# An FFT convolution on one core: the head's weight and pixel steps regrouped, and its loads reordered

## The chip, the core and the metric

The kernel runs on one core of a Trainium2 chip. The metric is the device time of one execution in microseconds; the time of the kernel before is the median of three runs. One further execution was taken with the hardware profiler, and the timelines below are from it. The engines are TensorE (PE: matrix products, with PEld for its weight loads), VectorE (DVE), ScalarE (ACT), GpSimd (POOL) and SyncE (SP), which issues the DMAs of this kernel. A "core's 16 DMA engines" move the data.

## The reference

```python
def reference(x, w):                       # x: 1 x 224 x 224 x 96, w: 7 x 7 x 96 x 96, bf16
    B, H, W, C = x.shape
    K = w.shape[0]
    wp = jnp.pad(w, ((0, H - K), (0, W - K), (0, 0), (0, 0)))
    Xf = jnp.fft.rfft2(x.astype(jnp.float32), axes=(1, 2))
    Wf = jnp.fft.rfft2(wp.astype(jnp.float32), axes=(0, 1))
    Yf = jnp.einsum('bhwi,hwio->bhwo', Xf, Wf)
    return jnp.fft.irfft2(Yf, s=(H, W), axes=(1, 2)).astype(jnp.bfloat16)
```

That is a circular convolution of a 224 x 224 picture of 96 channels with 7 x 7 weights, 96 channels in and 96 out.

## The kernel before, in words

The height is cut into NJ = 8 strips of 28 rows, which are transformed along the height only, with a short Fourier transform that gives NS = 17 frequencies (two of them, 0 and 16, are pairs of real ones: `REAL`). The strips are held in two groups (`jg`) of four, each 118 picture rows with its overlap of 6 rows. The width is cut into seven tiles of 32 pixels. Along the width the kernel convolves directly, two pixels (phases) at a time, with a scheme of ten tap planes (`NTAP`) in place of seven.

Four kinds of work follow each other:

- **Weights.** The 49 weights of every pair of channels lie in a wide SBUF tile `wq`, one weight per partition. There are two copies: rows 30 to 78 for output channels in full order, and rows 79 to 127 shifted by 48 channels, so that one matmul can serve two output channels. The matmul multiplies a strided column set of `wq` with the factor table `Em` (made at the start from a sine and masks), which gives the transformed weights in `WF`. The first group of frequencies (`wide_jobs`, L407, five frequencies in 11 slots) needs the first copy alone. The other groups (`prep_jobs`, L425, three frequencies each) need both. Each job is some matmuls into one PSUM bank and one eviction (a copy from PSUM to SBUF).
- **Pixels.** `f_jobs` (L514) transforms the pixels of the first three tiles, in three parts of the frequencies (`SH2`, 8 + 5 + 4), for each strip group; `a_bank` does the halo of three pixel pairs, and `a_jobs` the later tiles. The pixels come from DRAM by `load_rows` (L177), for each group one DMA of 112 rows (L183, `PAD` to `R`) and one of 6 rows.
- **Rounds.** `b_round` (L567) does one frequency of one tile: 33 matmuls (22 for a real frequency) on the pixel planes `xf` and the planes `J`, which DVE forms by `jit` (L536) for three frequencies at a time; then DVE and POOL combine the products into `yf`, which goes to DRAM (`scr`). The third slot of a frequency's weights is the difference of the first two (`diff`, L400, on DVE).
- **Way back.** `c_jobs` reads `scr` back into tiles `tt` (`load_t`, L673; its last group is read in parts of 64, 4 and 34 partitions), multiplies with a matrix `Gm` and stores the output.

What sets the order: each engine runs its instructions in the order in which the program writes them (`_Ordered`, L92). The head (L770 to L787) is written out by hand: 24 weight jobs of four channels, with the pixel transforms of tile 0's first part and the halo placed after the 12th, 16th and 20th, and a filler matmul (`warm`) after every fourth. The rounds follow (L828). Between the matmuls of a round other jobs are dealt out by `pace` (L795): a queue of jobs is entered with a first and a last step (`add(a, b, jobs)`), where round r of tile 0 has the steps 2r and 2r + 1. Weight group 1 is dealt from step 4 on, the second tile's first transform from step 3. `evac` (L133) gives each eviction to DVE or ACT, whichever has less by a running count.

SP issues its DMAs in order. The framework gives them eight semaphores in turn, so each DMA also waits until the eighth one before it has landed. In the head the order is (L203 to L213): the first weight copy (48 rows, then its last row in two DMAs of 16 pieces each), the first pixels of group 0, both halos, the first pixels of group 1, the second pixels of both groups, the second weight copy (48 rows in four DMAs by columns, then its last row).

Of the kernel before, what the change touches and what calls it, by code (L numbers as in the profile page):

```python
# [10 lines left out]
ALU = mybir.AluOpType  # L11
# [3 lines left out]
B = 28  # L15
L = B + KT - 1
LC = L - 2
NS = L // 2
REAL = (0, NS - 1)
JG = 4  # L20
# [8 lines left out]
NB0 = 4  # L29
# [4 lines left out]
PGRP = ((0, 5), (5, 8), (8, 11), (11, 14), (14, 17))  # L34
# [8 lines left out]
CQ = {2: (11, 0), 3: (11, 3), 4: (8, 7), 5: (4, 11), 6: (0, 11)}  # L43
SH2 = (0, 8, 13, 17)
# [3 lines left out]
FILL = 2  # L48
FEV = 4
WX0 = 12  # L50
WHALO = 16
WX1 = 20
W1 = 30
ZA = 1200
ZB = 3600
# [3 lines left out]
S5 = ((0, 1), (2, 3, 4), (5, 6, 11), (7, 8, 12), (9, 10, 13))  # L59
NW0 = 11  # L60


def slot(s, part):
    return S5[s][part] if s < len(S5) else 2 + 3 * (s - 1) + part


@with_exitstack
def kernel(
# [17 lines left out]
    assert K1 + PW == EP and len(S5) == PGRP[0][1]  # L86
# [26 lines left out]
    ps0_cm = tc.tile_pool(name="ps0", bufs=8, space=bass.MemoryType.PSUM)  # L113
    pools = {"psb": ps0_cm.__enter__()}
# [32 lines left out]
    def dma(out_ap, in_ap):  # L147
        return DE.dma_start(out=out_ap, in_=in_ap)
# [21 lines left out]
    Em = wqx[0:EP, WE:WE + 2 * NSLOT * NTAP].rearrange("p (h a t) -> p h a t", h=2, a=NSLOT)  # L170
# [6 lines left out]
    def load_rows(xb, jg, w0, npx):  # L177
        h0 = jg * HB - PAD
        n = npx * C

        def ld(p0, p1, hh):
            return dma(xb[p0:p1, 0:n], x[0, hh:hh + (p1 - p0), w0:w0 + npx, :].rearrange("h w c -> h (w c)"))
        return ld(PAD, R, h0 + PAD), ld(0, PAD, h0 % H)  # L183
# [9 lines left out]
    def load_w(p, k, n, h, m0=0, m1=C * C):  # L193
        return dma(wqx[p:p + n, m0:m1], bass.AP(wsrc.tensor, wsrc.offset + k * C * C + h * C2 + m0, [[C * C, n], [1, m1 - m0]]))

    def load_last(p, h):
        n = (C * C, WC)[h]
        m = n // 16
        for a, b in ((0, m // 2), (m // 2, m)):
            dma(wqx[p:p + 1, 0:n].rearrange("p (c m) -> p c m", c=16)[:, :, a:b],  # L200
                bass.AP(wsrc.tensor, wsrc.offset + (PW - 1) * C * C + h * C2 + a, [[C * C, 1], [m, 16], [1, b - a]]))

    load_w(W1, 0, PW - 1, 0)  # L203
    load_last(K1 - 1, 0)
# [3 lines left out]
    load_x(0, 1)  # L208
    for jg in range(2):
        load_x(1, jg)  # L210
    for i in range(4):
        load_w(K1, 0, PW - 1, 1, i * WC // 4, (i + 1) * WC // 4)
    load_last(EP - 1, 1)  # L213
# [5 lines left out]
    def warm(n):  # L219
        pwu = bank()  # L220
        for _ in range(n):
            TE.matmul(pwu[:].rearrange("p (a b) -> p a b", a=4), lhsT=wu[:, 0:128], rhs=wur, start=True, stop=True)
# [27 lines left out]
    zero_a(EP, WE // 2 + NSLOT * NTAP, 64 * C)  # L250
    zero_a(W1, 0, ZA)

# [31 lines left out]
    zero_a(W1, ZA, ZB)  # L284

    iota(twc[:], [[1, KT]])
    twp = ftile([EP, 1]); mk = ftile([EP, NTAP]); mk2 = ftile([EP, 2, NTAP])
# [7 lines left out]
    GE.memset(wz[0:W1, ZB:WE // 2], 0.0)  # L295
    GE.memset(mf[:], 1.0)
    GE.affine_select(out=mf[:], in_=mf[:], pattern=[[-B, JG], [0, NS * 2]], compare_op=ALU.is_ge, fill=0.0, base=-1, channel_multiplier=1)
    GE.affine_select(out=mf[:], in_=mf[:], pattern=[[B, JG], [0, NS * 2]], compare_op=ALU.is_ge, fill=0.0, base=LC, channel_multiplier=-1)
# [14 lines left out]
    pe3 = ftile([EP, NSLOT])  # L313
    pv = pe3[:, 2:].rearrange("p (s r) -> p s r", r=3)
    VE.tensor_copy(out=pe3[:, 0:2], in_=qe[:, 0, :])
    VE.tensor_single_scalar(out=pv[:, 0:NS - 2, 0], in_=qe[:, 1:NS - 1, 0], scalar=-2.0, op=ALU.mult)
    VE.tensor_tensor(out=pv[:, 0:NS - 2, 1], in0=qe[:, 1:NS - 1, 1], in1=qe[:, 1:NS - 1, 0], op=ALU.subtract)
    for r, k in ((0, KT - 1), (1, 0)):
        VE.tensor_single_scalar(out=pv[:, NS - 2, r:r + 1], in_=thp[:], scalar=float(k), op=ALU.is_equal)
    VE.tensor_tensor(out=pv[:, :, 2], in0=pv[:, :, 0], in1=pv[:, :, 1], op=ALU.subtract)  # L320

    def factors(h0, h1, out_ap, in_ap):
        n = list(in_ap.shape[1:])
        o, i = out_ap, in_ap.unsqueeze(len(n) + 1)
        m = mk2[:, h0:h1]
        if h1 - h0 > 1:
            i = i.unsqueeze(1)
            m = m.unsqueeze(2)
            shape = [EP, h1 - h0, *n, NTAP]
        else:  # L330
            m = m.unsqueeze(2) if len(n) > 1 else m
            shape = [EP, *n, NTAP]
        VE.tensor_tensor(out=o, in0=i.to_broadcast(shape), in1=m.to_broadcast(shape), op=ALU.mult)
    factors(0, 1, Em[:, 0, 0:5], pe3[:, 0:5])
    factors(0, 1, Em[:, 0, 5:NW0].rearrange("p (s r) t -> p s r t", r=2),
            pe3[:, 5:14].rearrange("p (s r) -> p s r", r=3)[:, :, 0:2])
    factors(0, 2, Em[:, :, NW0:], pe3[:, NW0:])
    factors(1, 2, Em[:, 1, 0:NW0], pe3[:, 0:NW0])
# [68 lines left out]
    def wide_jobs():  # L407
        ncol = NW0 * NTAP
        wcol = 512 // NB0
        assert ncol <= wcol and C % NB0 == 0  # L410

        def mk_(ob):
            def f():
                pw = bank()
                pv_ = pw[:].rearrange("p (k q) -> p k q", q=wcol)
                ev = Em[0:K1, 0].rearrange("p a t -> p (a t)")[:, 0:wcol]
                o0 = ob * NB0
                for k in range(NB0):
                    TE.matmul(pv_[:, k], lhsT=wqx[0:K1, o0 + k:o0 + k + 127 * C + 1:C], rhs=ev, start=True, stop=True)
                wv = WF[0:C, 0:NW0].rearrange("i a t o -> i (a t) o")  # L420
                apart(("W", 0), ob, evac(wv[..., o0:o0 + NB0], pv_[0:C, :, 0:ncol].rearrange("i k q -> i q k"), NB0 * ncol))
            return f
        return [mk_(ob) for ob in range(C // NB0)]

    def prep_jobs(gi):  # L425
        s0, s1 = PGRP[gi]
        ns = s1 - s0
        ncol = 2 * ns * NTAP
        nb = C // NB
        hb = NB // 2  # L430
        assert NB * ncol <= 512 and C2 % hb == 0

        def mk_(ob):
            def f():
                pw = bank()
                wv = WF[0:C, slot(s0, 0):slot(s1 - 1, 2) + 1]
                pv_ = pw[:, 0:NB * ncol].rearrange("p (k h q) -> p k h q", h=2, q=ncol)
                ev = Em[:, :, slot(s0, 0):slot(s1 - 1, 2) + 1, :]
                ev = ev.rearrange("p h (s r) t -> p h s (r t)", r=3)[:, :, :, 0:2 * NTAP]
                for k in range(hb):  # L440
                    o = ob * hb + k
                    TE.matmul(pv_[:, k], lhsT=wqx[0:EP, o:o + 127 * C + 1:C], rhs=ev, start=True, stop=True)
                pv_ = pv_[0:C]
                o0, o1 = ob * hb, (ob + 1) * hb
                wv = wv.rearrange("i (s r) t (h o) -> i s (r t) h o", r=3, h=2)
                apart(("W", gi), ob, evac(wv[:, :, 0:2 * NTAP, :, o0:o1],
                      pv_.rearrange("i k h (s q) -> i s q h k", s=ns), NB * ncol))
            return f
        return [mk_(ob) for ob in range(nb)] + [diff(s) for s in range(s0, s1) if s not in REAL]
# [64 lines left out]
    def f_jobs(t, part):  # L514
        s0, s1 = SH2[part], SH2[part + 1]
# [255 lines left out]
    fj = [f_jobs(0, p) for p in range(3)]  # L771
    warm(FILL)
    load["v"] += 900
    for i, f in enumerate(wide_jobs()):
        if i == WX0:
            for g in fj[0][0]:
                g()
        if i == WHALO:
            for jg in range(2):
                for g in a_bank(0, xf0, xh_bufs[jg], 0, 3, jg, 0):  # L780
                    g()
        if i == WX1:
            for g in fj[0][1] + jit(0, 0):
                g()
        f()
        if i % FEV == FEV - 1:
            warm(1)  # L787
# [25 lines left out]

    for gi in range(1, len(PGRP)):
        add(4 if gi == 1 else 2 * PGRP[gi - 1][0], 2 * PGRP[gi - 1][1] - 1, prep_jobs(gi))
# [12 lines left out]
    for r in range(NS + LAG):  # L828
        if r == 0:
            for i in range(2, PGRP[0][1]):  # L830
                add(2 * i - 3, 2 * i - 2, [diff(i)])
            add(1, 6, fj[1][0] + fj[1][1])
            add(6, 10, fj[2][0] + fj[2][1])
        if r == 2:
            new_xf(1, SH2[0], SH2[1])
        for p in range(3):
            if r == (1, 3, 5)[p]:
                if p:
                    new_xf(1, SH2[p], SH2[p + 1])
                else:  # L840
                    xf_tiles[1] = xf_bufs[1]
                fj = f_jobs(1, p)
                if p == 2:
                    for jg in range(2):
                        fj[jg][-1] = then_load(fj[jg][-1], 2, jg)
                add(2 * r + 1, 2 * r + (5, 5, 4)[p], fj[0] + fj[1])
# [144 lines left out]
```

## Time and profile before

| | us |
|---|---|
| median of three runs | 272.68 (270.92 to 272.82) |
| profiled execution, its time | 269.92 |
| its span | 268.2 |
| first weight matmul / first matmul of a round | 8.17 / 19.39 |
| PE's longest wait in the rounds, for the second weight copy | 2.65, up to 26.82 |
| all bytes moved by the DMA engines | 46.78 MB, 174 GB/s on average |

A line of the timeline gives the start, the duration, the engine (a "q" behind it: its instruction queue, where DMAs are issued), the line of the program, the operation, what is written and read, how many instructions were merged into the line, and in brackets the idle time before it with what ended it. All work of this kernel goes through one helper, so every line has the number L102, and groups are told apart by their tiles: `pb` is a PSUM bank, `WF` the transformed weights (the tile's end also holds the first pixels), `wq` the raw weights, `xn` the pixels, `xf` the transformed pixels, `wu` the filler. The trace also keeps, for each DMA, the times at which its semaphore was raised, and a record of every packet.

### The profile page before, as it was taken

What the parts mean: (1) busy time and instruction counts of PE and PEld (TensorE: products, weight loads), DVE (VectorE), ACT (ScalarE), POOL (GpSimd) and SP (SyncE); (2) the same over time, 40 slices, a digit from 0 to 9 for tenths busy, and PEclk for the clock granted to TensorE, in tenths of its full rate; (3) what the DMA queues carried; (4) which work ended last, traced back from release to release, by engine and by line L of the source; (5) the groups of instructions that cost most, each with busy time, mean ns of one, the idle gap of its engine ahead of it and who ended that gap; (6) DMA issues with size and microseconds to landing.
All of it is one profiled execution on the core that took longest, in us unless ns stands there. A gap on an engine that the chain in (4) does not pass through costs nothing.

```text
span 268.2 us, 12140 instructions
## 1 busy us (share of the span) xinstructions
PE 254.2 (95%) x5127; PEld 235.4 (88%) x5127; DVE 216.0 (81%) x463; ACT 198.1 (74%) x487; POOL 99.8 (37%) x153
## 2 busy tenths in 40 slices
PE   8786999999999999999999999999999999999983
PEld 2775999989998999999999998989999889879862
DVE  7896799989899788779787888787898889878614
ACT  8686897487974578988988789887987864178113
POOL 7784215363647435322322222224123332422100
PEclk9999999999999999999999999999999999999999
DMA  7995101811111598987967387979788434787866
GB/s 162 250 242 94 50 2 46 241 51 66 46 46 50 161 260 138 290 268 197 297 184 218 110 212 249 236 186 350 267 155 240 169 108 143 196 235 197 233 123 205
DMA packets 46882, 46.78 MB, mean 174 GB/s; under 512 B 35340, under 2 KB 38104, under 8 KB 46780
## 3 DMA queue, kind: packets, MB, share of 16 engines
q1 hardware_dynamic: 44540, 43.95, 59.7%
q10 hardware_dynamic: 2288, 2.06, 2.7%
q8 instruction: 40, 0.66, 1.0%
q14 instruction: 14, 0.11, 0.1%
HBM read 24.66 MB, written 21.33 MB: 171 GB/s over the span
## 4 chain that ended last, share of the span: by engine, by line
PE 66%; DMA 16%; DVE 10%; ACT 2%; issue 2%; SPq 1%; DVEq 0%; ACTq 0%
PE pb L102 66%; DVE J L102 4%; DMA scrb<-yf 4%; DMA xn<-in_x_dram 3%; DMA wq<-in_w_dram 3%; DMA WF<-in_x_dram 3%; DMA tt<-scr 2%; DVE WF L102 2%; DVE v L102 2%; DMA xf<-scrb 1%; DVE u L102 1%; ACT xf L102 1%; SPq L102 1%; DVE yf L102 0%; ACT J L102 0%
## 5 line engine op out<-in xcount | busy, mean ns | idle before, releaser
L102 PE MATMUL pb<-WF,J 96*128 96x96 bf16 x2821 | 162.7, 206 | 1.8 <-DVE J L102 1.1
L102 PEld LDWEIGHTS <-J 96*128 96x128 bf16 x2821 | 138.0, 98 | 12.1 <-issue 3.5
L102 POOL TENSOR_TENSOR yf<-v,u 128x384 bf16<-128x384 f32 x79 | 81.6, 1044 | 144.4 <-issue 84.7
L102 ACT CAST xf<-pb 96x408 bf16<-96x408 f32 (+3 forms) x146 | 67.5, 486 | 6.4 <-PE pb L102 2.7
L102 PE MATMUL pb<-WF,xf 96*128 96x96 bf16 x952 | 59.9, 206 | 1.1 <-ACT WF L102 1.1
L102 DVE TENSOR_TENSOR J<-xf 96x456 bf16<-96x456 bf16 (+3 forms) x85 | 56.8, 708 | 0.1
L102 PEld LDWEIGHTS <-xf 96*128 96x128 bf16 x952 | 47.1, 98 | 1.5 <-issue 1.4
L102 PE MATMUL pb<-Fm,xn 118*128 118x136 bf16 (+3 forms) x640 | 45.5, 199 | 0.0
L102 PE MATMUL pb<-tt,Gm 102*84 102x384 bf16 (+1 forms) x132 | 32.8, 327 | 0.2
L102 ACT CAST WF<-pb 96x480 bf16<-96x480 f32 (+1 forms) x59 | 28.7, 557 | 4.2 <-PE pb L102 4.2
L102 PEld LDWEIGHTS <-xn 118*128 118x128 bf16 x640 | 30.1, 97 | 0.0
L102 ACT CAST J<-pb 84x384 bf16<-84x384 f32 (+1 forms) x64 | 27.6, 490 | 2.6 <-PE pb L102 2.6
L102 ACT CAST yo<-pb 84x384 bf16<-84x384 f32 (+1 forms) x64 | 27.5, 487 | 2.3 <-POOL yf L102 1.3
L102 PE MATMUL pb<-wq 128*128 128x120 bf16 (+1 forms) x288 | 21.8, 226 | 4.3 <-DMA wq<-in_w_dram 2.6
L102 DVE TENSOR_TENSOR J<-J 96x912 bf16<-96x912 bf16 (+2 forms) x42 | 24.3, 579 | 0.0
L102 PEld LDWEIGHTS <-wq 128*128 128x128 bf16 (+1 forms) x288 | 19.8, 148 | 5.1 <-issue 2.8
L102 DVE TENSOR_TENSOR yf<-v,u 128x384 bf16<-128x384 f32 x26 | 14.7, 566 | 0.9
L102 PE MATMUL pb<-wu 128*112 128x384 bf16 (+1 forms) x58 | 13.8, 385 | 1.1 <-DVE J L102 1.1
L102 PEld LDWEIGHTS <-wu 128*112 128x112 bf16 (+1 forms) x58 | 7.2, 126 | 5.6 <-issue 2.8
L102 PEld LDWEIGHTS <-Gm 102*84 102x84 bf16 (+1 forms) x132 | 11.1, 117 | 0.9 <-issue 0.2
L102 ACT COPY xf<-xf 96x816 bf16<-96x816 bf16 (+3 forms) x20 | 11.1, 612 | 0.0
L102 ACT CAST tt<-pb 112x384 bf16<-112x384 f32 x8 | 3.6, 480 | 9.7 <-PE pb L102 9.5
(391 smaller groups left out, 243.4 us busy)
## 6 DMA issues: line engine op xcount, KB each, us to landing
scr<-yf SPq DMA_DIRECT2D x30, 288.0 KB
xn<-in_x_dram SPq DMA_DIRECT2D x12, 672.0 KB
tt<-scr SPq DMA_DIRECT2D x24, 336.0 KB
out_dram<-yo SPq DMA_DIRECT2D x12, 252.0 KB
out_dram<-J SPq DMA_DIRECT2D x12, 252.0 KB
tt<-scr SPq DMA_DIRECT2D x6, 288.0 KB
WF<-in_x_dram SPq DMA_DIRECT2D x2, 672.0 KB
out_dram<-tt SPq DMA_DIRECT2D x8, 168.0 KB
```

Source lines behind the costliest of these rows:

```text
L102: r = fn(*a, **k)
```

## The change

In the head, weights go in jobs of twelve channels instead of four, each into a PSUM tile of two banks with one eviction; the first weight group has four frequencies in 8 slots instead of five in 11, and the first pixel transform six frequencies instead of eight. The order of the head's steps is a list, `HEAD`, and the filler matmul goes ahead of each weight job but the first. The factor table is stored in stripes in the spare end of `wq`. The zeroing of `wq` is split by output half, all on ACT, the second half later. The second weight copy is loaded ahead of the second pixels; both copies' order changes: the last row of the first copy goes first, and the second copy is loaded in DMAs of all 49 rows. Pixel rows that do not wrap round the picture (group 1) are loaded in one DMA of 118 rows. Work that leaves the head goes into the rounds: weight groups are now 4 + 3 + 3 + 3 + 4, the last in jobs of six channels.

```diff
-NB0 = 4
+NB0 = 12
-PGRP = ((0, 5), (5, 8), (8, 11), (11, 14), (14, 17))
+PGRP = ((0, 4), (4, 7), (7, 10), (10, 13), (13, 17))
+SH0 = (0, 6, 13, 17)
+HEAD = ("w", "w", "w", "w", "x0", "w", "h0", "w", "h1", "w", "w", "x1")
...
-S5 = ((0, 1), (2, 3, 4), (5, 6, 11), (7, 8, 12), (9, 10, 13))
+S4 = ((0, 1), (2, 3, 8), (4, 5, 9), (6, 7, 10))
...
-    ps0_cm = tc.tile_pool(name="ps0", bufs=8, space=bass.MemoryType.PSUM)
+    psh_cm = tc.tile_pool(name="psh", bufs=4, space=bass.MemoryType.PSUM)
...
+        if h0 >= 0:
+            return ld(0, R, h0)
         return ld(PAD, R, h0 + PAD), ld(0, PAD, h0 % H)
...
+    load_last(K1 - 1, 0)
     load_w(W1, 0, PW - 1, 0)
-    load_last(K1 - 1, 0)
     load_x(0, 0)
     for jg in range(2):
         load_rows(xh_bufs[jg], jg, W - PAD, PAD)
     load_x(0, 1)
+    for i in range(4):
+        load_w(K1, 0, PW, 1, i * WC // 4, (i + 1) * WC // 4)
     for jg in range(2):
         load_x(1, jg)
-    for i in range(4):
-        load_w(K1, 0, PW - 1, 1, i * WC // 4, (i + 1) * WC // 4)
-    load_last(EP - 1, 1)
...
-    zero_a(EP, WE // 2 + NSLOT * NTAP, 64 * C)
-    zero_a(W1, 0, ZA)
+    zero_a(EP, WE // 2, 64 * C)
+    zero_h(0, 0, ZC)
...
+    zero_h(0, ZC, C)
+    late_zero = zero_h(1, 0, C)
...
         def mk_(ob):
             def f():
-                pw = bank()
+                pw = psum_tile()
...
+                if ob:
+                    warm(1, pw)
                 for k in range(NB0):
-                    TE.matmul(pv_[:, k], lhsT=wqx[0:K1, o0 + k:o0 + k + 127 * C + 1:C], rhs=ev, start=True, stop=True)
+                    o = ob * NB0 + k
+                    m = TE.matmul(pw[:, k // nk, k % nk * ncol:(k % nk + 1) * ncol], lhsT=wqx[0:K1, o:o + 127 * C + 1:C],
+                                  rhs=ev, start=True, stop=True)
...
+    def head_x(jg):
+        s1 = SH0[1]
+        fv = Fm[:, :, 0:s1].rearrange("p r s j -> p r (s j)")
+        n = 2 * s1 * JG
+        for ph in range(2):
+            pa = psum_tile()
+            for k in range(TW):
+                i = 2 * k + ph
+                TE.matmul(pa[:, k // 8, k % 8 * 64:k % 8 * 64 + n], lhsT=xbuf(0, jg)[:, i * C:i * C + 128], rhs=fv, start=True, stop=True)
+            xo = xf0[0:C, ph, :, 0:s1, HALO:HALO + TW, jg * JG:(jg + 1) * JG]
+            pi = pa[0:C].rearrange("c b (w q) -> c (b w) q", q=64)[:, :, 0:n].rearrange("c w (r s j) -> c r s w j", r=2, s=s1)
+            apart(("A", 0), (0, jg, ph, 0), evac(xo, pi, TW * n))
...
-        nb = C // NB
-        hb = NB // 2
+        nb = C // (NB if 2 * ncol * (NB // 2) <= 512 else 6)
+        hb = C2 // nb
...
+    wj = wide_jobs()
+    for h in HEAD:
+        if h == "w":
+            wj.pop(0)()
+        else:
+            (head_x if h[0] == "x" else head_h)(int(h[1]))
+    for g in jit(0, 0):
+        g()
...
-        add(4 if gi == 1 else 2 * PGRP[gi - 1][0], 2 * PGRP[gi - 1][1] - 1, prep_jobs(gi))
+        add(3 if gi == 1 else 2 * PGRP[gi - 1][0], 2 * PGRP[gi - 1][1] - 1, prep_jobs(gi))
...
-            add(1, 6, fj[1][0] + fj[1][1])
-            add(6, 10, fj[2][0] + fj[2][1])
+            add(0, 4, fj[1][0] + fj[1][1])
+            add(8, 12, fj[2][0] + fj[2][1])
...
-            if r == (1, 3, 5)[p]:
+            if r == (1, 3, 6)[p]:
...
-                add(2 * r + 1, 2 * r + (5, 5, 4)[p], fj[0] + fj[1])
+                add((4, 7, 12)[p], (7, 11, 15)[p], fj[0] + fj[1])
```

## The prediction, made before the changed kernel ran

> **What bounds it now.** I read the page's engine rows first, then the timeline of PE, then that of SP, then the DMA view and the trace's semaphore records.
>
> ```profile
> PE 254.2 (95%) x5127; PEld 235.4 (88%) x5127; DVE 216.0 (81%) x463; ACT 198.1 (74%) x487; POOL 99.8 (37%) x153
> q1 hardware_dynamic: 44540, 43.95, 59.7%
> 8.17 1.19 PE L102 MATMUL pb<-wq 79*128 79x128 bf16 x16 [1.62 <-POOL ct L102]
> 19.39 0.50 PE L102 MATMUL pb<-WF,xf 96*128 96x96 bf16 x8 [1.15 <-ACT WF L102]
> 26.82 0.92 PE L102 MATMUL pb<-wq 128*128 128x120 bf16 x12 [2.65 <-DMA wq<-in_w_dram]
> ```
>
> TensorE sets the time. The reader is to see in the three timeline rows when the head starts (8.17), when the rounds start (19.39), and the one long wait in the rounds: at 26.82 PE had waited 2.65 us (2.81 from the last start) for the second weight copy. After that, gaps between matmul starts, beyond the usual pitch, sum to about 5 us up to the tail. So any shift of the round start, and any new wait of PE, goes to the end in full. The DMA engines are 60% busy, with room only if the work is spread evenly. Each DMA uses the 16 engines as its shape allows, and the change alters two shapes.
>
> ```profile
> 0.80 1.70 SPq L102 DMA_DIRECT2D wq<-in_w_dram  x3
> 2.54 6.06 SPq L102 DMA_DIRECT2D WF<-in_x_dram  x8
> 10.24 1.50 SPq L102 DMA_DIRECT2D xn<-in_x_dram  x4
> 11.78 7.58 SPq L102 DMA_DIRECT2D wq<-in_w_dram  x6
> ```
>
> These are SP's issues in the head: first weights, first pixels, second pixels, second weights. The first packet leaves 1.04 us after its issue (0.80 to 1.83), and a landing is recorded about 1.1 us after its last packet (6.44 to 7.59).
>
> **The step that decides: 118 and 49 rows.** Every engine that carries a part of a DMA raises its semaphore once; where fewer than 16 do, one more rise comes at once, about 0.5 us after the issue. Counted in the trace: 112, 128 and 48 rows give 16 late rises; 84, 56 and 28 rows give 14; 18 rows 9; 12 rows 12; 6 rows 6; 4 rows 4; and the 34-row pieces of tt (L684) only 2. Each count is the largest divisor of the row number that is at most 16. The changed code loads pixel group 1 in one DMA of 118 rows (2 x 59) where L183 has 112 + 6, and the second weights in DMAs of 49 rows (7 x 7) where L212 has 48. So I take **two engines for 118 rows and seven for 49.** The two 34-row pieces, issued 0.32 us apart at 120.45, land 1.3 us apart, near the 1.4 us that 68 packets of 384 B take at 20 ns: they run one behind the other on the same two engines. The Trainium skill, "DMA: Bandwidth & Descriptors", section "Why a DMA increments its semaphore by 16 and not by 1", gives this rule (largest k up to 16 that divides the slowest dimension, on the lowest-numbered engines); the trace agrees wherever it has a row, but has none for 118 or 49.
>
> What a row costs:
>
> ```profile
> DMA packets 183, 0.99 MB, mean 283 GB/s; under 512 B 22, under 2 KB 22, under 8 KB 183
> q1 hardware_dynamic: 183, 0.99, 96.6%
> ```
>
> That is 92.5 to 96 us, mostly one pixel load: 0.99 MB in 16 x 3.5 x 0.966 engine-us is 18.3 GB/s each, 0.336 us for a row of 6144 B. From 14 to 20 us it is 1.42 MB at 99.9%, or 0.415 us a row. The packet records have 0.234 at the fast tenth. With two engines alone drawing, I take 0.25 us, near the fast end; 0.234 and 0.415 stay as bounds.
>
> **Head, on the two engines, in the new order.** The two pieces of the last weight row go first (0.64 + 0.58 us of SP), so the 48 rows are issued at about 2.1 and start at 3.1. Three packets of 1.27: 6.9. First pixels, 8 rows at 0.40: 10.1. Halos: 8 packets of 0.076, then group 1's halo, now 118 rows, 59 x 0.076 = 4.5: 15.2. First pixels of group 1: 59 x 0.25 = 14.8: 30.0, landed **31.1**. Second weights, 4 x 7 packets of 4.6 KB at 0.2 (0.184 fastest, 0.37 in the head): 35.6. Second pixels, group 0: 37.6; group 1, again 14.8: 52.4, landed **53.5**. It was 21.4 before.
>
> PE reaches the last head step (transform of group 1) about 9.2 us after its first matmul, near 18, and waits to 31.1. Then 32 matmuls at 29 ns, the last eviction of 768 elements (0.93 us by DVE's 0.64 for 512), the first J piece (0.47); the second weights are landed when the first prep job asks for them. The next stop is the fifth job of the second pixels' first transform, the first one on group 1, in step 5 of the rounds. Up to there PE has done 88 convolution matmuls x 0.043, 64 first-pixel ones x 0.028, 36 weight ones x 0.0625 and 32 second-pixel ones x 0.029: 8.8 us, and stands at about 42. It goes on at 53.5. Before, the same work (8.6 at its pitches) was done at 19.4 + 8.6 + 2.8 = 30.8. **Shift +22.7.** The bounds: 0.234 a row and every other row at its fastest end at +18.8; 0.415 and 0.37 at +47.
>
> PE after a long pause: sixteen 512-column matmuls at the start take 5.50 us, the first ten 0.427 apart, the later 0.216. A pause of 2.65 us brought no such slow run. Pauses of 9 to 13 us are not in the trace: 0 to 10 x 0.211 = 2.1 us each, so 0 to 4.2; I take **+1**, as the first pause is followed by waits on evictions anyway. The Trainium skill, "TensorE: Matmul & The Clock Gate", section "Part 1: The HAM clock gate", halves the clock after an idle window of 3.4 us, for about as long: by it, an estimate of 1.7 us each; no run here shows it yet.
>
> **Later tiles: five more 118-row loads.** The trace gives issue and first use of group 1 for the tiles after: 49.5 to 67.3, 93.1 to 109.0, 123.1 to 138.9, 157.9 to 170.8, 184.9 to 203.2: 17.9, 16.0, 15.8, 12.9, 18.3 us.
>
> ```profile
> 157.86 0.83 SPq L102 DMA_DIRECT2D xn<-in_x_dram  x2
> 170.77 0.34 PE L102 MATMUL pb<-Fm,xn 118*128 118x136 bf16 x3
> ```
>
> The new load takes 1.0 + 59 x 0.27 (a middle of the later windows) + 1.1 = 18.0. Short by 0.1, 2, 2.2, 5.1 and 0. Behind it on the same two engines stand loads of tt. For tile 2 they are issued from 96.06 and first used at 103.92; behind a load that ends at 93.1 + 17 they land at 111: 7 us instead of 2. Every DMA on SP also waits for the landing of the eighth before it, so SP stops eight issues behind a slow load; for the other three tiles I add 2 to 3 us each. Together about 0.5 + 7 + 4 + 7 + 3 = **+21.5.** Cross-check: per tile the two engines carry 59 x 0.27 in place of 8 x 0.27, 13.8 us more on some 21 now (48 store packets of 0.09, 420 gather packets of 0.022, 24 output packets of 0.12, 16 rows), 35 in periods of 28 to 33: +2 to +7 per tile. Bounds 0 (all hidden) and +40 (0.35 a row, every shortfall 5 us more).
>
> **All other edits** are covered by these waits: two-bank evictions, 12,384 elements in 14 evictions for 16,288 in 36; one weight group of four instead of three (16 evictions for 12); factors in stripes; zeroing on ACT. Their cost if the cover is gone is in rival 1. A two-bank eviction is not in the trace: a plain extrapolation gives 1.13 us (DVE) and 0.92 (ACT) for 960, a second start would add 0.13; 14 of them leave PE's wait for 31.1 as it is.
>
> **Sum.** The profiled execution took 269.92 (span 268.2). 269.9 + 22.7 + 1 + 21.5 = 315.1. It lies 2.76 below the median of the three runs, 272.68, so **318** against that median.
>
> **Rivals.** (1) The rows spread over all engines, and the change does what it says. Then the second weights land near 19 and the 2.81 wait goes. Against it: the first weights start 1.3 later with no small pieces behind them (0.45): +0.6; PE stays bound in the head, 96 weight matmuls at 0.0625 whether 120 or 128 columns, so hardly less at 80, and J now follows the last eviction: +0.8; +0.5 of PE work in the rounds, about +0.5 of new waits as 1 us per engine of evictions moves there. 272.7 - 2.8 + 2.4 = 272.3, not slower. It decides if a 118-row DMA uses eight engines or more; only the lack of such a row in the trace speaks for it. (2) Two engines, but the later loads hide: 18 us against slacks of 13 to 18 speaks for it, tt behind them against: 272.7 + 23.7 = 296. (3) Two engines at crowded pace throughout, 0.415 in the head and 0.35 later: 272.7 + 47 + 40 = 360; the busy windows speak for it, the fast tenth against.
>
> **Chances.** Forecast 0.60 (303 to 335), rival 2 0.23, rival 3 0.13, rival 1 0.04. Range: from rival 2's lower edge, 291, to 352, which leaves out most of rival 3 and all of 1. A measurement of this kernel tells about 1% from no change: slower 0.96, within 0.03, faster 0.01, the last two from rival 1.
>
> **What would show it.** Right: the 118-row loads with two late rises, group 1's first transform starting near 31 after a wait on a DMA, a second wait of about 10 us ending near 53, then waits at tt or xn once per tile; GB/s near 50 in 18 to 50 us. Wrong: sixteen rises for 118 rows, or rounds starting near 20.

## The result and the profile after

The changed kernel takes **341.0 us** (median of six runs, 339.99 to 343.31) against 272.1 (six runs, 270.92 to 273.45): a ratio of 1.254, 95% interval 1.248 to 1.260. The profiled execution took 340.27, its span is 338.5. The forecast was 318, its range 291 to 352.

The page of the changed kernel, the lines that answer to those shown of before (engine: busy time, share of the span, instructions; queue: packets, MB, share of the engines' time), and the two rows of slices (8.46 us each):

```profile
span 338.5 us, 12099 instructions
PE 272.0 (80%) x5126; PEld 250.1 (74%) x5126; DVE 215.4 (64%) x459; ACT 202.5 (60%) x474; POOL 97.3 (29%) x152
PEclk9585696999998999679999999956999699999998
GB/s 139 163 133 53 57 82 5 5 124 105 85 41 37 40 154 118 108 162 281 206 95 133 198 181 193 84 107 209 216 306 86 49 218 277 132 158 236 201 187 163
q1 hardware_dynamic: 44284, 43.95, 44.8%
```

The same two rows of the kernel before (slices of 6.71 us):

```profile
PEclk9999999999999999999999999999999999999999
GB/s 162 250 242 94 50 2 46 241 51 66 46 46 50 161 260 138 290 268 197 297 184 218 110 212 249 236 186 350 267 155 240 169 108 143 196 235 197 233 123 205
```

The same 43.95 MB go through SP's queue, but the engines are busy 44.8% of the time with it instead of 59.7%. A low rate alone says little: before, too, it is 46 to 66 GB/s where little is to be moved. New are low rates while loads are pending: 53 and 57 GB/s in the slices from 25 to 42 us. A row of 6144 B takes 0.238 us where such a load runs alone (40 to 50 us), so two engines move an estimated 52 GB/s. PE falls from 95% to 80%. Before, its granted clock is 0.9 or more in every slice; after, it shows fives to sevens at PE's waits and just behind them.

PE's timeline in the head, the rows with a wait:

```profile
9.27 0.99 PE L98 MATMUL ps<-wq 79*128 79x80 bf16 x12 [3.09 <-DMA wq<-in_w_dram]
30.38 1.46 PE L98 MATMUL ps<-Fm,WF 118*128 118x48 bf16 x32 [10.69 <-DMA WF<-in_x_dram]
32.89 0.80 PE L98 MATMUL pb<-WF,xf 96*128 96x96 bf16 x8 [1.05 <-DVE xf L98]
51.22 1.03 PE L98 MATMUL pb<-Fm,xn 118*128 118x64 bf16 x16 [6.29 <-DMA xn<-in_x_dram]
```

PE waits 10.69 us for the first pixels of group 1 and 6.29 us for the second. The rounds start at 32.89 instead of 19.39. The wait for the second weight copy (2.65 at 26.82 before) is gone.

The later tiles, in the chain that ended last (start, duration, what):

```profile
126.72 17.53 DMA tt<-scr
...
167.22 18.27 DMA scr<-yf
...
209.45 18.19 DMA out_dram<-yo
...
253.77 15.17 DMA scr<-yf
```

Each of these four is issued 0.5 to 5.7 us after a 118-row load (123.68, 165.56, 208.98, 248.12) and lands 0.8 to 2.8 us after it. None of them is the load itself.

To see where the time lies I cut PE's row of matmuls at fixed marks of the program and split each piece, by the distance from one matmul's start to the next: work at the usual pitch of that kind of matmul, what the slower pitch adds, and gaps.

| piece, up to | its time before, us | after, us | more | slower pitch more | gaps more |
|---|---|---|---|---|---|
| second pixels of group 1 begin | 30.0 | 51.2 | +21.2 | +4.5 | +16.3 |
| second tile's last first-part transform | 19.3 | 22.6 | +3.3 | +2.1 | -0.2 |
| third tile done | 43.6 | 49.7 | +6.1 | +1.7 | +6.1 |
| end of tile 6's transform | 122.2 | 161.5 | +39.3 | +6.3 | +33.0 |
| the end | 48.7 | 48.7 | 0 | 0 | 0 |
| sum | | | +69.9 | +14.6 | +55.2 |

What the two last columns leave of a row is work that moved from one piece to another; over the kernel the work is the same, about 245 us by this split. The whole loss is waits, and slow matmuls after waits.

### The profile page after: what moved, and what is told of

It reads as the page before. It is cut to its first block, busy times and chain, and to the rows that moved or that the text cites. A ratio compares the mean times of both kernels' runs of the same rounds, so it can differ in the third digit from the quotient of the medians.

```text
span 338.5 us, 12099 instructions
## 1 busy us (share of the span) xinstructions
PE 272.0 (80%) x5126; PEld 250.1 (74%) x5126; DVE 215.4 (64%) x459; ACT 202.5 (60%) x474; POOL 97.3 (29%) x152
## 3 DMA queue, kind: packets, MB, share of 16 engines
q1 hardware_dynamic: 44284, 43.95, 44.8%
## 4 chain that ended last, share of the span: by engine, by line
PE 35%; DMA 27%; DVE 7%; ACT 3%; issue 1%; DVEq 0%; SPq 0%; ACTq 0%
PE pb L98 35%; DMA scr<-yf 12%; DMA tt<-scr 8%; DMA out_dram<-yo 5%; DVE J L98 3%; DVE v L98 2%; ACT WF L98 1%; DMA scrb<-yf 1%; DVE WF L98 1%; DVE yf L98 1%; DMA xf<-scrb 1%; DVE u L98 1%; ACT J L98 1%; ACT xf L98 1%; ACT yo L98 0%
## 5 line engine op out<-in xcount | busy, mean ns | idle before, releaser
L98 PE MATMUL pb<-WF,J 96*128 96x96 bf16 x2821 | 170.4, 210 | 23.2 <-ACT yo L98 17.1
L98 PEld LDWEIGHTS <-J 96*128 96x128 bf16 x2821 | 144.6, 100 | 36.3 <-issue 23.2
L98 ACT CAST xf<-pb 96x408 bf16<-96x408 f32 (+4 forms) x137 | 64.4, 491 | 14.3 <-PE pb L98 11.1
L98 PE MATMUL pb<-WF,xf 96*128 96x96 bf16 x952 | 62.9, 211 | 1.0 <-DVE xf L98 1.0
L98 PEld LDWEIGHTS <-xf 96*128 96x128 bf16 x952 | 49.8, 101 | 1.2 <-issue 0.7
L98 ACT CAST WF<-pb 96x480 bf16<-96x480 f32 x46 | 28.5, 722 | 1.4 <-PE pb L98 1.4
L98 PEld LDWEIGHTS <-Gm 102*84 102x84 bf16 (+1 forms) x132 | 11.4, 120 | 11.6 <-issue 10.3
L98 PE MATMUL pb<-wq 128*128 128x120 bf16 (+1 forms) x192 | 16.3, 232 | 1.3 <-ACT WF L98 1.0
L98 PEld LDWEIGHTS <-WF 118*128 118x128 bf16 x204 | 8.7, 111 | 10.8 <-DMA WF<-in_x_dram 10.8
L98 PE MATMUL ps<-Fm,WF 118*128 118x48 bf16 (+1 forms) x76 | 4.0, 217 | 10.7 <-DMA WF<-in_x_dram 10.7
L98 DVE CAST xf<-ps 96x768 bf16<-96x768 f32 (+1 forms) x4 | 3.9, 979 | 11.8 <-PE ps L98 11.7
```

What stands on the lines that cost most here:

```text
L98: r = fn(*a, **k)
```

## The experiments

Two families start from the changed kernel: with its loads cut back to row numbers that spread, and then with the 118-row loads given back in one place at a time. A third starts from the kernel before. Ratios are against the kernel before on the same chip.

### a_split: the changed kernel, with rows that divide well

Pixels go as 112 + 6 rows again, the second weights as 48 + 1. All other edits stay.

```diff
-        if h0 >= 0:
-            return ld(0, R, h0)
         return ld(PAD, R, h0 + PAD), ld(0, PAD, h0 % H)
...
-        load_w(K1, 0, PW, 1, i * WC // 4, (i + 1) * WC // 4)
+        load_w(K1, 0, PW - 1, 1, i * WC // 4, (i + 1) * WC // 4)
+    load_last(EP - 1, 1)
```

> The changed kernel with only the row counts of its DMAs put back: pixel group 1 in 112 + 6 rows, second weights in 48 rows and a last row in 16 pieces. Theory (the 118- and 49-row DMAs, on two and seven engines, make the loss): 272 to 279 us, sixteen late rises for each large load, PE's long waits gone; what is left over 272 is the dearer evictions of the last weight group (3 channels wide), which in the changed kernel stood before PE waits of about 6 us near 85 to 106. Rival (the regrouped head and rounds carry much of the loss): 300 us or more.

Measured: 282.35 us (281.9 to 282.84), ratio 1.0422 (1.0369 to 1.0474). So 59 of the 69 us go with the two row numbers. But some 11 are left where the prediction's first rival put none (272.3), and the run misses its own expected window. The trace has no wait for the second weights any more, as that rival said. In its place PE's pitch is slower (12.0 us against 6.5) and the gaps are longer (18.1 against 11.6), mostly between 62 and 105 us, where nothing is loaded late. The further runs on this base look for that.

### a_117: is it the row number, or the single DMA?

As a_split, but the pixels of group 1 go as 117 + 1 rows: almost the same long DMA, and 117 = 13 x 9.

```diff
+        if h0 >= 0:
+            return ld(0, R - 1, h0), ld(R - 1, R, h0 + R - 1)
```

> As the run before, but group 1 in 117 + 1 rows. By the largest divisor up to 16, 117 = 9 x 13 goes on thirteen engines, nine rows each instead of seven: within 2 us of the run before, thirteen late rises. Rival (any row number that is no multiple of 16 is slow, or falls to two engines): over 300 us.

Measured: 281.47, ratio 1.0384 (1.0332 to 1.0436), the same as a_split. The semaphore records show 13 late rises for 117 rows, 2 for 118, 7 for 49. Against the changed kernel one row less in the pixel DMA, with the second weights in 48 + 1 rows, takes 59 us off. Long DMAs are not slow as such; the number of rows decides. What the 49 rows cost by themselves no run shows; b_118 below has the 118 alone. The Trainium skill, "DMA: Bandwidth & Descriptors", section "Why a DMA increments its semaphore by 16 and not by 1", takes the largest divisor up to 16; these three new counts agree.

### a_late118 and a_head118: the two places apart

First the 118-row load for tiles 2 to 6 alone, then for tiles 0 and 1 and the halo alone (with the 49-row weights).

```diff
+        if h0 >= 0 and npx == 2 * TW and w0 >= 4 * TW:
+            return ld(0, R, h0)
```

> 118 rows kept only for the five loads of tiles 2 to 6; head loads in 112 + 6, second weights in 48 + 1. Theory: the head is as in the run with all counts put back, the waits of the later tiles stay: that run + 35 to 48 us, 310 to 325. Rival (the later loads hide, and their waits in the changed kernel came from the disturbed head): that run + 0 to 10.

```diff
+        if h0 >= 0 and (npx == PAD or w0 < 4 * TW):
+            return ld(0, R, h0)
```

> 118 rows only for the loads of tiles 0 and 1 and the halo, second weights in 49; later tiles in 112 + 6. Theory: PE's waits up to 30 and 51 us stay, later ones go: the run with all counts put back + 18 to 24 us, 292 to 302. Both parts together should give about the 341 of the changed kernel. Rival (the head's loss is regained later behind other limits): + under 10.

Measured: 321.64 (320.52 to 322.75), ratio 1.1869, for the later tiles: **+39.3** over a_split, where the prediction had +21.5. And 300.53 (300.24 to 300.82), ratio 1.109, for the head: **+18.2**, where it had +23.7 (counted from the kernel before, whose second pixels begin 2.4 us earlier than a_split's). 282.35 + 39.3 + 18.2 = 339.9: the parts add up to the changed kernel.

What PE waited for in the first of these (wait: total, times, longest), and three pieces of its chain:

```profile
PE pb L98 <- ACT yo L98: 16.6, 2, 9.9
PE pb L98 <- DMA tt<-scr: 9.7, 2, 9.5
...
PE pb L98 <- DMA xn<-in_x_dram: 2.6, 1, 2.6
```

```profile
147.20 18.20 DMA xn<-in_x_dram
...
191.16 17.01 DMA out_dram<-yo
...
234.23 14.97 DMA scr<-yf
```

The late pixels themselves cost PE 2.6 us. The other waits come from what is queued behind them: a gather of `tt` (9.5), and output stores. An output store that takes 17.01 us (in a_split 1.7 to 6.6) keeps its `yo` buffer, ACT cannot evict into it, the PSUM bank stays full, and PE stops: 16.6 us under the name of ACT. These waits are 28.7 of the 39.3 us; most of the other 10 are slower matmuls behind them (from 105 us to the end of tile 6's transform the granted clock is 0.87 on average, in a_split 1.00). By tiles, the profiled execution is later than that of a_split by 0 (tile 2), 11.9 (3), 5.5 (4), 11.8 (5) and 11.9 (6, with the tail); predicted were 0.5, 7, 4, 7 and 3.

### a_late_act: the same late loads on another queue

As a_late118, but ScalarE's instruction stream issues the five loads.

```diff
-            return ld(0, R, h0)
+            return SE.dma_start(out=xb[0:R, 0:n], in_=x[0, h0:h0 + R, w0:w0 + npx, :].rearrange("h w c -> h (w c)"))
```

> As a_late118 (118-row loads of pixel group 1 in tiles 2 to 6 alone, 321.6), but these five loads are issued on ScalarE's DMA queue instead of SyncE's. Two theories of the 39 us that they cost. Theory Q: the stores and gathers issued after a load on the same queue stand behind its 59 rows on the same two engines' rings; another queue has rings of its own, so they pass it, and only the load's own lateness is left (18 us against slacks of 12.9 to 18.3, some 10 us in all): 290 to 305. Theory E: the two engines themselves are full, or SyncE still stops at the landing of the eighth DMA before; the ring does not matter: 315 to 328, with the same waits of PE for scr, tt and out_dram in the trace.

Measured: 337.06 (337.03 to 337.10), ratio 1.2414 (1.2336 to 1.2491): slower still, and outside both windows. A row from the waits of PE, and one from those of SP's queue:

```profile
PE pb L98 <- ACT J L98: 20.9, 3, 10.6
```

```profile
SPq L98 <- DMA xn<-in_x_dram: 59.4, 5, 20.9
```

Theory Q holds for the stores. SP still issues five while one of these loads is under way. Four of them land 6.7 to 8.6 us after issue, ahead of the load (the fifth is issued 2.5 us before the load's end); in a_late118 the stores behind a load take 15 to 18.5, in tile 2 12.4. It fails for the gathers. Tile 3's is still 18.8 us from issue to landing, and PE waits 10.83 for it. The packet records of that gather, in two of its microseconds (S is SP's queue, A ScalarE's; packets begun):

```
us          a_late118 (all on S)    a_late_act
118 - 119   9 of 6144 B             8 of 6144 B (A), 8 of 384 B (S)
119 - 120   9 of 6144 B             8 of 6144 B (A), 8 of 384 B (S)
```

With one queue the two engines finish the 59 rows first (to 122) and then the gather. With two they take one packet of each in turn, and a 384-byte packet costs a turn like a 6144-byte row. From 115 to 122 that goes on at the same 8 of each in a us. A store of `scr` (288 KB in packets of 2304 B) has 8 packets for each of 16 engines and passes; a gather (336 KB in packets of 384 B) has 56, nearly as many as the load has rows for each of its two engines, and comes through no sooner than the load.

Theory E holds for the rest, and more strongly than it said: of SP's five waits for pixels (59.4 us in all) three, of 16.3, 16.7 and 20.9 us, end when one of ScalarE's loads has landed. Each time SP waits for the semaphore that this load has: the eight go round over both queues, and the next DMA that gets the same one is not issued before. Stores that are not yet issued are as late as stores that stand behind. What this second wait would cost with a semaphore of its own for the load stays open: that was not tried.

The Trainium skill, the same page, section "Queues, rings and completion order", says that every DMA engine goes round between the queues that have work on it, a packet at a time; the packet records agree.

### a_grp2: where 8 of the remaining 11 us are

In a_split the evictions of the last weight group (four frequencies, six output channels in a job, so three channels side by side for each half) stand out. ACT's timeline of a_split, an earlier group with four channels side by side, then the last group:

```profile
60.64 1.46 ACT L98 CAST WF<-pb 96x480 bf16<-96x480 f32 x3
66.28 3.48 ACT L98 CAST WF<-pb 96x480 bf16<-96x480 f32 x4
```

The same 480 elements take 0.49 us each in the first row (1.46 / 3) and 0.87 in the second (3.48 / 4). So the frequencies were grouped so that every job has runs of four:

```diff
-PGRP = ((0, 4), (4, 7), (7, 10), (10, 13), (13, 17))
+PGRP = ((0, 4), (4, 6), (6, 8), (8, 11), (11, 14), (14, 17))
```

> The run with all row counts put back, 282.35 us, still 12 over the kernel before, so the counts are not all of the loss. New theory: 6.3 us of PE waits and some 2.5 of slow pace near 62 to 90 us come from the last weight group, whose evictions write runs of three channels (six bytes) and take 0.7 to 0.95 us each on ACT where runs of four take 0.44. This kernel has weight groups 4, 2, 2, 3, 3, 3 in place of 4, 3, 3, 3, 4, so that every run is four channels; it has 24 evictions of 320 elements for 16 of 480. Theory: 273 to 276. Rival (it is the volume moved out of the head, not the width of the runs): 281 to 284, as volume and count do not fall.

Measured: 274.42 (273.68 to 274.87), ratio 1.0142 (1.0090 to 1.0194): 7.9 us less than a_split, though there is one weight group more. The gaps between 62 and 105 us are gone (18.1 to 10.4 us over the kernel).

### a_hb2: narrow runs, or odd ones?

As a_split, with the last group in jobs of four channels: runs of two, 24 evictions of 320 elements in place of 16 of 480.

```diff
-        nb = C // (NB if 2 * ncol * (NB // 2) <= 512 else 6)
+        nb = C // (NB if 2 * ncol * (NB // 2) <= 512 else 4)
```

> As a_split (282.4), but the last weight group (four frequencies) in jobs of two channels a half, 24 evictions of 320 elements, instead of 16 of 480 with three channels. Theory odd: an inner run of three bf16 (6 bytes) is what makes these evictions slow (0.7 to 0.95 us where runs of four take 0.44); runs of two would then go at the usual cost per element, some 0.35 us each, and the run comes to 274 to 278. Theory short: the cost goes by the number of runs, so 2 x 80 x 2 = 160 runs of four bytes per... eviction cost as much as 160 runs of six bytes, 24 of them in place of 16: slower than a_split, 284 to 292.

Measured: 279.26 (276.10 to 280.14), ratio 1.0258 (1.0187 to 1.0329), between the windows, and nearer to that of theory odd. ACT's timeline in its last group:

```profile
66.41 2.53 ACT L98 CAST WF<-pb 96x320 bf16<-96x320 f32 x6
```

About 0.42 us each, but 24 of them. The first eviction of a burst, which waits for nothing, can be compared across the runs (ACT): 0.422 us for 320 elements in 80 runs of four (a_grp2), 0.531 for 320 in 160 runs of two (the first two bursts; in the later ones the recorded time grows to 0.77, while one still starts every 0.39), 0.543 for 480 in 120 runs of four, 0.897 for 480 in 160 runs of three. From the first two, a run costs 1.4 ns; by that, 480 elements in 160 runs would take 0.543 + 40 x 1.4 ns = 0.60. The other 0.30 us belong to the three. DVE has the same order: 0.477, 0.530, 0.644, 0.908. So runs of three bf16 are slow beyond their number; the place in the program is not it, as runs of two are written in the same place. Why three are slow these runs do not show.

### a_fill and a_grp2_fill8: the head's slow matmuls

In a_split PE pauses 3.03 us before the first weights (1.62 before), and the next weight matmuls are slow; its clock is 0.75 in 10 to 20 us. First, twelve more fillers on a_split to cover the pause:

```diff
     xf0 = new_xf(0)
+    warm(12)
```

> The run with all row counts put back, with twelve more filler matmuls after the first fourteen, so that PE stands idle about 0.5 us ahead of the first weight matmul instead of 3.0. Theory: the 3.0 us pause makes PE run at half pace up to about 15 us and again after 20 (granted clock 0.75 and 0.83 there, 1.00 in the kernel before), which the matmul starts put at 2.5 to 3 us; expected 279.0 to 280.5, granted clock near 1.00 from 10 to 20 us. Rival (the evictions set the head's pace, PE's clock is hidden): 282 within 0.7.

Measured: 282.84 (282.48 to 283.78), ratio 1.0453: no gain. The fillers do what they should: the clock is 1.00 from 10 to 20 us, and the rounds start at 20.25 instead of 21.55. Then PE stops. Its timeline:

```profile
20.25 0.50 PE L98 MATMUL pb<-WF,xf 96*128 96x96 bf16 x8 [1.31 <-DVE xf L98]
22.74 0.33 PE L98 MATMUL pb<-WF,xf 96*128 96x96 bf16 x4 [0.22 <-DVE WF L98]
28.80 0.22 PE L98 MATMUL pb<-WF,xf 96*128 96x96 bf16 x1 [2.76 <-issue]
```

The stop of 2.76 us has no releaser ("issue"). A packet of 16 KB on the instruction queue starts at 26.30 and takes 1.15 us, in the middle of it, while pixels fill the same engines (a_split has that packet at 24.92). That PE waited for its own instructions is argued from this, not shown.

Then on a_grp2, with seven fillers, and the first copy's 48 rows issued ahead of its single last row again:

```diff
-    load_last(K1 - 1, 0)
     load_w(W1, 0, PW - 1, 0)
+    load_last(K1 - 1, 0)
...
     xf0 = new_xf(0)
+    warm(7)
```

> As a_grp2 (274.4: short rows in place of 118 and 49, six weight groups with runs of four channels), with the first weights' 48 rows issued ahead of the single last row again and seven more filler matmuls ahead of the first weight job, so that TensorE does not stand still there. If the rest of the loss over the kernel before (3.1 us) is the pause of 3.0 us and the half pace after it, plus the later first weights: 270.5 to 273. If, as in a_fill, what the fillers win is lost again at a stop of TensorE's own instruction stream some 15 us later: 273.5 to 275.

Measured: 271.89 (270.48 to 273.15), ratio 1.0015 (0.9983 to 1.0048), inside the first window: no difference from the kernel before is left. It too has a stop of 1.74 us without releaser, up to 27.0.

### b_118: the one row number on the kernel before

```diff
+        if h0 >= 0:
+            return ld(0, R, h0)
         return ld(PAD, R, h0 + PAD), ld(0, PAD, h0 % H)
```

> The kernel before with one thing changed: group 1 of pixels and halo in one DMA of 118 rows. Theory: the loss of the 118 rows does not need the rest of the change; first pixels of group 1 land near 27 to 31, the second near 50 to 55, later tiles as in the run with 118 only there: 325 to 340. Rival (it needs the new order of the loads to hurt the head): 305 to 320.

Measured: 340.84, one run, 0.8 above its window. Two lines in the kernel before cost as much as the whole change. The second long stop of its head is 9.25 us for the second weights: here they are queued behind the 118 rows of the second pixels (landed at 47.6) and land at 50.3. By the same cut, its head is 4.4 us worse than that of the changed kernel (second pixels of group 1 begin at 55.6, not 51.2) and its later tiles and end some 6 us worse; the changed kernel in turn loses 9.4 between these (+3.3 and +6.1 in the table). The equal totals are two different sums.

### b_w2first and b_w2fill: the one useful part, alone

In the kernel before, only the order of the loads is changed: second weights ahead of the second pixels. Then the same with nine fillers instead of two.

```diff
-    for jg in range(2):
-        load_x(1, jg)
     for i in range(4):
         load_w(K1, 0, PW - 1, 1, i * WC // 4, (i + 1) * WC // 4)
     load_last(EP - 1, 1)
+    for jg in range(2):
+        load_x(1, jg)
```

> The kernel before with one thing changed: the second weight copy is loaded ahead of the second pixels, all in its own row counts. The 2.81 us wait for the weights goes. The second pixels, 1.45 MB, now land last, near 22 to 25 us, and their first job stood at 22.7. Theory: half of the wait comes back at that job, net 0 to -2 us, 268.5 to 271 on a kernel before of 270.6. Rival one: the whole wait goes, -2.8. Rival two: the pixels are as late as the weights were and two groups must land, +0 to +2.

```diff
-FILL = 2
+FILL = 9
```

> As b_w2first (the kernel before with the second weights loaded ahead of the second pixels, 270.0), with seven more filler matmuls ahead of the first weight job. If its head was lost to half pace after the pause of 2.6 us before the first weights, the rounds start near 19.5 instead of 21.3 and the run takes 267 to 269. If the head is bound by something else (evictions, or the refill of TensorE's instructions as in a_fill), it stays at 269.5 to 271.

Measured: 269.97 (268.52 to 271.43, ten runs), ratio 0.9954 (0.9921 to 0.9987), and 269.75 (268.76 to 271.20, twelve runs), ratio **0.9936 (0.9911 to 0.9960)**. The first is inside the window of its theory (half of the wait comes back). PE's timeline of the first, then of the second:

```profile
8.56 1.20 PE L102 MATMUL pb<-wq 79*128 79x128 bf16 x16 [2.54 <-POOL WF L102]
21.29 0.50 PE L102 MATMUL pb<-WF,xf 96*128 96x96 bf16 x8 [1.15 <-ACT WF L102]
25.45 0.63 PE L102 MATMUL pb<-Fm,xn 118*128 118x64 bf16 x16 [0.66 <-DMA xn<-in_x_dram]
```

```profile
19.68 0.50 PE L102 MATMUL pb<-WF,xf 96*128 96x96 bf16 x8 [1.21 <-ACT WF L102]
21.84 0.30 PE L102 MATMUL pb<-WF,J 96*128 96x96 bf16 x3 [1.20 <-issue]
25.16 0.63 PE L102 MATMUL pb<-Fm,xn 118*128 118x64 bf16 x16 [0.62 <-DMA xn<-in_x_dram]
```

The wait of 2.65 for the second weights is gone in both. In the first, a pause of 2.54 before the first weights is followed by slow matmuls (clock 0.66 in 10 to 15 us; the rounds start at 21.29). In the second the clock is 1.00 there and the rounds start 1.6 us earlier, as expected, but the total misses its window of 267 to 269: both meet again at 25.45 and 25.16, where the second pixels have just landed. So the loads bound this stretch now, and the second's gain over the first is no more than their intervals. (The profiled executions, 271.43 and 268.76, are further apart than the medians; behind 25 us that is within the spread of one kernel's runs.) It is the fastest version here, 0.6% under the kernel before.

## Why the prediction was right, and where it was not

| step | predicted | measured |
|---|---|---|
| engines for 118 and 49 rows | 2 and 7 | 2 and 7 |
| first pixels of group 1 landed | 31.1 | 30.3 |
| second pixels of group 1 landed | 53.5 | 51.2 |
| shift at that point | +22.7 | +21.2 |
| slow matmuls after the pauses | +1 | +4.5 within the shift above, +2.1 in the next piece, +14.6 in all |
| later tiles | +21.5 | +39.3 |
| all other edits | 0 | +6.1 behind the head's waits; 11 without them |

The measured 341.0 lies inside the range, but above the forecast's own band (303 to 335). The deciding step was right; the sum came out 23 too low because three of its terms were too small: the later tiles, the slow matmuls and the other edits.

**The deciding step held**, and a_117 and b_118 show that it is the cause. The row's cost too: in the later tiles the loads land 16.8 to 18.0 us after issue, predicted 18.0. The second stop was 6.29 us instead of about 10: the pixels landed 2.3 us earlier, and PE got there at 44.9 (51.22 - 6.29) instead of 42, its matmuls in between being slow.

**The later tiles are the term that was mis-sized**, +39.3 for +21.5 with the bound at +40. For the gather of `tt` behind a load, 7 us were worked out in tile 3, and PE's wait measured 9.5 to 9.7. The step that failed is the "2 to 3 us each" for SP and the queue on the other tiles. It counted the load's own shortfall and a standing SP; the stores of `scr` and `yo` on the same two engines' queue, whose buffers hold ACT and then PE, were not priced. They held ACT for up to 11.4 us at a time in a_late118, 12.7 in the changed kernel. The cross-check through the two engines' occupation (+2 to +7 per tile) was no check: the engines were not full, the queue was in order.

**The clock** was taken as two pauses of the head, +1 within 0 to 4.2. There are five waits of 6 us or more, and PE runs slowly after them: +14.6 over the kernel, +6.3 of it inside the later tiles' 39.3. The Trainium skill, "TensorE: Matmul & The Clock Gate", section "Part 1: The HAM clock gate", gave an estimate of 1.7 us a wait, so an estimate of 8.5 for five: nearer than the value taken.

**"All other edits cost nothing under cover"** was true only of the head. The six-channel jobs of the last weight group run at 82 to 106 us, where PE waits for no load, and cost there in the changed kernel (+6.1 in the table) as well as in a_split (7.9 by a_grp2). The prediction gave evictions by their elements (0.92 us for 960 on ACT; measured 0.965) and never asked how many elements lie side by side.

**Rival 1** (272.3 with spread rows) is answered by a_split and a_grp2: 282.4, and 274.4 once the runs of three are gone. Of its terms, the -2.8 for the second weights came as -2.2 (the gaps of PE up to the second pixels, 2.8 before, 0.6 in a_split); +0.6 for the first weights was +0.9 and, through the pause, some 1.5 of slow matmuls more. **Rival 2** (later loads hide, 296) fell with a_late118; **rival 3** (crowded rows, 360) had the total closer in the later tiles but for the wrong reason, as a row took its 0.26 us ((17.4 - 1.0 - 1.1) / 59) there.

## What to carry to other kernels

Count the divisors of a DMA's row number before joining two transfers: 112 + 6 rows in two DMAs took 5 to 7 us here where 118 in one took 17, and 117 + 1 was as good as 112 + 6. Price a slow transfer by what stands behind it in its queue, by which buffers those hold and by who must wait for its semaphore; its own first use cost 2.6 of 39 us, and another queue made it worse. For an eviction, look at the innermost run as well as the element count.

## What the runs showed of the hardware that was not expected

- Evictions with runs of three bf16 took 0.90 us (ACT) and 0.91 (DVE, one eviction) for 480 elements, 0.54 and 0.64 with runs of four; runs of two cost only 0.11 and 0.05 more than runs of four at 320 elements.
- Pauses of 2.54 and 3.03 us ahead of the first weights brought slow matmuls (granted clock 0.66 and 0.50 in 10 to 15 us; about 1.5 us more from the first weights to the rounds in both), and with the pause filled they went; one of 1.62 there, and one of 2.65 at 26.82 in the kernel before, brought none. The Trainium skill, in the section on the clock named above, wants an idle window of 3.4 us; two pauses here were shorter and still slowed PE.
- Two engines shared by two queues changed packet by packet, 8 of 384 B and 8 of 6144 B in the same microsecond: what a small transfer waits beside a large one goes by its number of packets, not by its bytes.
- When the head was made faster by fillers, PE stopped for 1.2 to 2.8 us with no releaser, 1 to 6 us into the rounds, in all three kernels with more fillers. A late refill of its instructions would fit in a_fill and a_grp2_fill8, where a 16 KB packet of the instruction queue lies in the stop or runs into it; in b_w2fill none lies in it (the last ends at 20.32, the stop lasts from 20.65 to 21.84). The cause stays open.
